# Softcap attention and a maxout MoE on one core: a new order of work, with each attention visit in one piece and all weight subtractions on VectorE

## The chip, the cores and the metric

The kernel runs on one core of one Trainium2 chip. The time is the device time of one execution in microseconds (us); the number before the change is the median of three runs. Engines are named as in the profile: PE is TensorE (PEld its weight loads), DVE is VectorE, ACT is ScalarE, POOL is GpSimd, SP is SyncE.

## What is computed

```python
def _attn_ref(q, k, v, cap):                       # (8, 12, 448, 64) each
    scale = 1.0 / np.sqrt(q.shape[-1])
    scores = scale * np.matmul(q, k.transpose(0, 1, 3, 2))
    scores = cap * np.tanh(scores / cap)           # cap = 30
    scores = scores - np.max(scores, axis=-1, keepdims=True)
    attn = np.exp(scores)
    attn = attn / (np.sum(attn, axis=-1, keepdims=True) + 1e-09)
    return np.matmul(attn, v).astype(np.float32)

def _moe_ref(x, w1, w2, w_out):                    # x: (3584, 768), w1, w2: (768, 1024)
    h1 = x @ w1
    h2 = x @ w2
    g = np.maximum(h1, h2)
    return (g @ w_out).astype(np.float32)          # w_out: (1024, 768)
```

The attention's output, heads side by side, is the x of the second part.

## The kernel before, in words

**The algebra.** max(h1, h2) is relu(x (w1 - w2)) + x w2, so the second part is relu(x wd) w_out + x wm with wd = w1 - w2 and wm = w2 w_out. wd is made by six subtractions, one for each chunk of 128 rows (`subtract`, L354; step `sub`). wm is made by transposing w2 on PE (`W`, L368; copied by `WC`, L372) and multiplying it with w_out (`OP`, `P`, L383; copied by `PC`, L389).

**The attention** works on 48 pairs of heads i = 0..47. Two pairs, 2t and 2t + 1, make a visit t = 0..23, four heads. For each pair, three passes of scores (`S i j`, L466) fill one of two score tiles s0 and s1 in PSUM with 128 keys x two heads x 448 queries; ACT reads the tile with a tanh (`T i j`, L471, 128x896) and then takes the exponent in place in pieces of one, two or three passes (`E i j0 j1`, L488). The last 64 keys of all four heads are one pass of the visit (`L`, L480), with a tanh (`TL`, L484) and an exponent (`EL`, L491). The maximum is not subtracted. The values are `VL t` (last keys, L552) and `V t u j0 j1` (L558), where u is the half of the head's 64 columns. They accumulate in a score tile too, so the tile is taken until the result is normalized. The denominators: DVE adds the exponents of the three passes and the rest (`A t ab j`, L500, and `B t half`, L505), PE sums them over the keys (`Y t`, L525; the first three visits sum all exponents on PE, L518 and L522), and DVE turns, inverts and turns back (`Y1`, `Y2`, `Y3`, L530 to L536) and multiplies into xT (`N t 0`, L570, and twice in `N t 1`, L573). `Y` uses one of four `mm` banks of PSUM.

**The second part** runs over 120 groups, 30 for each pair of batches: `stage1` (8 for each batch, six chunks of wd, evicted with a relu by DVE, L622) and `stage2` (14 halves for a pair of batches, 14 chunks each, copied to osb by DVE, L658, or near the end by ACT, L656). A group opens with `O g bank`. `M x y n` does n steps, each one 64-row half of a chunk of group x in the lower half of the rows of PE and one of group y in the upper half, side by side (L597). `M g g n` takes whole chunks (L592). A group has to change from its one half to its other by a hand-over: an empty instruction on SP (`Hs g`) or DVE (`H g`) waits for the first half's last matmul, and the group's next half waits for it. `ev g` evicts a group (`eva g` on ACT), `st b t` stores an output tile from SP.

**Loads.** POOL issues all loads but the first two, in its order of the list: `lk`, `lq`, `lv` (k, q, v), `lw1`, `lw2`, `lwo` (weights; w1 arrives as f32, in the memory of later osb tiles for chunks 0 to 3 and of a later xT tile for 4 and 5). For the first ten pairs PE transposes q and k (`X`, L410, copied by `XC`, L415); afterwards SP does so with a DMA (`cr t`, L427). There are two buffers each of the loaded q and k, of the transposed ones and of v. `D` are matmuls on a tile of zeros that keep PE going until data come (L423).

**The order of the work** is the string ORDER: its steps are executed as they stand, so it is each engine's queue, in order. An engine waits for data and for free buffers by semaphores and never overtakes its own queue. Nothing else in the program sets an order.

Of the kernel before, what the change touches and what calls it, by code (L numbers as in the profile page):

```python
# [9 lines left out]
ld0 k; ld0 q; ms0; dm; cd k; lk 1 0; lq 1 0; lw2 3; lk 2 0; lw2 2; id; lq 3 0; lq 2 0; lw2 0; lw2 1; lk 3 0;  # L10
D 3 16; cd q; D 3 15; Xh 0 0 0; Xh 0 1; D 3 4; XCh 0 0; XCh 0 1; D 3 4; S 0 0; D 3 5; S 0 1; D 3 4; T 0 0; T 0 1;
D 3 4; S 0 2; D 3 12; X 1 1; D 3 16; W 3 2; XC 1; ms; WC 3; L 0; T 0 2; E 0 0 3; TL 0; S 1 2; D 3 8; X 2 2; S 1 0;
D 3 8; W 2 0; D 3 4; T 1 2; T 1 0; S 1 1; E 1 2 3; T 1 1; XC 2; S 2 1; D 3 1; W 1 3; X 3 2; S 2 0; W 0 1; lk 4 0;
lq 4 0; lwo 0 0; lwo 0 1; lv 0 0; lv 0 1; lk 6 0; lwo 1 0; lwo 1 1; lq 5 0; lv 1 1; lk 7 0; lq 6 0; lk 5 0; lw2 5;
lq 7 0; lv 1 0; T 2 1; T 2 0; WC 1; XC 3; WC 2; WC 0; L 1; X 4 2; S 2 2; OP 2 0 0; P 2 0 1; OP 1 0 1; P 1 0 3;
OP 0 0 3; P 0 0 2; P 1 0 1; P 0 0 1; P 2 0 1; P 0 0 1; P 2 0 2; P 1 0 1; P 2 0 3; P 1 0 3; P 2 0 1; TL 1; EL 0;
T 2 2; EL 1; E 1 0 2; XC 4; PC 2 0; PC 1 0; S 3 0; VL 0; V 0 1 0 2; Y 0 0; V 0 0 0 3; V 0 1 2 3; Y1 0; Y2 0; Y3 0;
N 0 1; N 0 0; T 3 0; E 2 0 3; S 3 1; OP 2 1 2; P 2 1 2; OP 1 1 0; P 1 1 1; OP 0 1 1; P 0 1 1; P 0 0 1; P 1 1 2;
P 0 1 3; P 0 0 2; P 2 1 2; P 1 1 1; P 0 0 1; S 3 2; T 3 1; E 3 0 2; T 3 2; S 4 0; P 0 1 2; P 1 1 2; P 0 1 2;
P 2 1 3; P 1 1 1; S 4 1; T 4 0; E 3 2 3; T 4 1; PC 0 1; PC 0 0; S 4 2; X 5 1; OP 3 0 3; P 3 0 2; P 2 1 1; P 1 1 1;  # L20
XC 5; PC 2 1; PC 1 1; L 2; W 5 1; T 4 2; TL 2; VL 1; V 1 0 0 1; Y 1 0; V 1 0 1 3; V 1 1 0 3; S 5 0; Y1 1; Y2 1;
WC 5; Y3 1; lv 2 1; lw2 4; lk 8 0; lq 9 0; lq 8 0; lw1 0; lw1 2; lk 9 0; lv 2 0; E 4 0 3; T 5 0; X 6 0; XC 6;
N 1 0; N 1 1; P 3 0 3; S 5 1; OP 3 1 2; P 3 1 1; W 4 0; P 3 0 3; P 3 1 7; S 5 2; EL 2; T 5 1; E 5 0 2; T 5 2;
WC 4; PC 3 1; PC 3 0; sub 0 0; S 6 0; OP 4 0 0; P 4 0 8; X 7 3; S 6 1; PC 4 0; XC 7; sub 2 0; T 6 0; E 5 2 3;
T 6 1; S 6 2; X 8 2; X 9 0; L 3; T 6 2; TL 3; Y 2 3; VL 2; S 7 0; V 2 1 0 1; EL 3; T 7 0; XC 8; XC 9; Y1 2; lw1 1;
lw1 5; lk 10 1; lw1 3; lw1 4; lk 12 1; lk 10 0; lq 11 0; lv 3 0; sub 5 1; lv 3 1; lk 11 0; lk 11 1; lq 10 0;
V 2 1 1 2; V 2 0 0 3; V 2 1 2 3; OP 5 0 3; P 5 0 1; OP 4 1 0; P 4 1 2; OP 5 1 2; P 5 1 1; S 7 1; P 4 1 2; P 5 1 3;
P 4 1 1; P 5 1 1; P 5 0 4; P 4 1 1; P 5 0 3; P 5 1 3; P 4 1 2; E 6 0 3; T 7 1; Y2 2; Y3 2; sub 1 0; N 2 1; N 2 0;
sub 3 0; PC 5 0; PC 5 1; sub 4 0; S 7 2; S 8 0; E 7 0 2; T 7 2; T 8 0; O 0 1; M 0 -1 1; O 1 3; M 1 -1 2; M 0 -1 3;
S 8 1; M 0 -1 2; M 1 -1 1; S 8 2; Hs 0; cr 5; T 8 1; T 8 2; E 7 2 3; M 1 0 3; O 2 2; M 2 0 3; L 4; VL 3; A 3 1 1;  # L30
A 3 0 1; A 3 0 2; B 3 0; B 3 1; PC 4 1; A 3 1 2; TL 4; V 3 0 0 3; V 3 1 0 3; Y 3 0; S 9 0; M 2 1 3; ev 0; Y1 3;
Hs 2; EL 4; T 9 0; E 8 0 3; O 3 0; M 3 1 3; M 3 2 3; Hs 3; lv 4 1; lv 4 0; lq 12 0; lv 5 0; lk 13 0; lk 13 1;
lk 12 0; lq 13 0; lk 15 0; lv 6 3; lv 5 2; lk 14 1; lk 15 1; lq 14 0; lk 14 0; lv 5 3; lq 15 0; lv 5 1; S 9 1;
O 4 1; M 4 2 3; M 4 3 3; Y2 3; Y3 3; ev 1; N 3 0; ev 2; T 9 1; Hs 4; O 5 3; M 5 3 3; M 5 4 3; O 6 2; M 6 4 3;
ev 3; N 3 1; A 4 0 1; ev 4; Hs 5; M 6 5 3; O 7 0; M 7 5 2; S 10 0; Hs 6; M 7 5 1; M 7 6 1; S 9 2; M 7 6 2; Hs 7;
cr 6; E 9 0 2; T 10 0; T 9 2; E 9 2 3; O 8 1; M 8 6 3; S 10 2; M 8 7 3; S 10 1; A 4 1 1; ev 5; A 4 0 2; H 8;
B 4 1; B 4 0; A 4 1 2; ev 6; T 10 1; T 10 2; O 9 3; M 9 7 3; M 9 8 5; L 5; M 9 8 2; VL 4; V 4 1 0 2; Y 4 2;
V 4 0 0 3; V 4 1 2 3; TL 5; E 10 0 3; ev 7; Y1 4; Y2 4; Y3 4; N 4 1; N 4 0; S 11 0; M 9 8 4; O 10 0; M 10 8 3;
Hs 9; Hs 8 2; T 11 0; EL 5; M 10 9 3; M 8 9 2; S 11 1; M 8 9 4; S 11 2; M 8 9 2; O 11 2; M 11 9 1; T 11 1; T 11 2;
E 11 0 2; M 11 9 2; S 12 0; M 11 10 5; S 12 1; M 11 10 6; T 12 1; T 12 0; E 11 2 3; A 5 0 1; ev 8; O 12 1;  # L40
M 12 10 3; cr 7; Hs 11; H 10 2; A 5 1 1; ev 9; A 5 0 2; B 5 1; B 5 0; M 12 11 3; M 10 11 1; L 6; M 10 11 2;
S 12 2; M 10 11 5; ev 10; A 5 1 2; TL 6; T 12 2; O 13 3; M 13 11 3; S 13 0; M 13 12 4; VL 5; Y 5 0; V 5 1 0 3;
V 5 0 0 3; T 13 0; E 12 0 3; M 13 12 4; S 13 1; M 13 12 3; lv 6 0; lk 17 0; lv 6 1; lk 16 0; lk 17 1; lv 7 0;
lv 7 3; lq 16 0; lq 17 0; lk 16 1; lk 19 1; lv 6 2; Y1 5; Y2 5; Y3 5; N 5 0; N 5 1; ev 11; T 13 1; EL 6; E 13 0 2;
Hs 13; O 14 0; M 14 12 3; M 14 13 1; S 14 0; M 14 13 2; Hs 12 2; Hs 14; S 13 2; M 12 13 8; O 15 2; M 15 13 3;
M 15 14 3; T 13 2; T 14 0; E 13 2 3; A 6 0 1; A 6 0 2; ev 12; A 6 1 1; ev 13; Hs 15; st 0 1; cr 8; O 16 1;
M 16 14 1; S 14 1; M 16 14 2; M 16 15 3; O 17 3; M 17 15 3; S 14 2; T 14 1; T 14 2; B 6 1; H 16; ev 14; B 6 0;
A 6 1 2; ev 15; M 17 16 3; O 18 0; M 18 16 3; L 7; VL 6; V 6 1 0 3; Y 6 2; V 6 0 0 3; TL 7; S 15 0; M 18 17 3;
lv 8 2; lk 19 0; lq 19 0; lv 7 1; lk 18 1; lq 18 0; lk 18 0; lv 8 1; lk 21 0; lk 20 1; lk 20 0; lv 7 2; lv 8 3;
lk 21 1; ev 16; Y1 6; Y2 6; Y3 6; N 6 0; Hs 18; O 19 2; M 19 17 3; M 19 18 3; ev 17; N 6 1; EL 7; T 15 0;  # L50
E 14 0 3; Hs 19; S 15 1; O 20 1; M 20 18 3; M 20 19 3; O 21 3; M 21 19 3; S 15 2; ev 18; A 7 0 1; A 7 0 2; ev 19;
T 15 1; E 15 0 2; T 15 2; Hs 20; st 0 0; M 21 20 3; Hs 21; S 16 0; O 22 0; M 22 20 3; M 22 21 3; O 23 2;
M 23 21 3; Hs 22; cr 9; ev 20; A 7 1 1; ev 21; M 23 22 6; S 16 1; M 23 22 5; O 24 1; M 24 22 3; T 16 0; E 15 2 3;
T 16 1; B 7 0; H 23; H 22 2; B 7 1; A 7 1 2; S 16 2; M 24 23 3; M 22 23 1; L 8; T 16 2; TL 8; M 22 23 7; S 17 0;
VL 7; Y 7 3; V 7 1 0 2; V 7 0 0 3; V 7 1 2 3; lv 9 2; lq 21 0; lq 20 0; lv 9 0; lv 8 0; ev 22; Y1 7; Y2 7; EL 8;
T 17 0; E 16 0 3; O 25 3; M 25 23 2; S 17 1; M 25 23 1; M 25 24 4; Y3 7; N 7 1; ev 23; N 7 0; M 25 24 7; O 26 0;
M 26 24 2; st 0 2; Hs 25; M 26 24 1; M 26 25 3; S 17 2; T 17 1; E 17 0 2; T 17 2; Hs 24 2; Hs 26; M 24 25 4;
S 18 0; M 24 25 4; O 27 2; M 27 25 3; M 27 26 5; S 18 1; T 18 0; E 17 2 3; T 18 1; M 27 26 1; S 18 2; M 27 26 5;
L 9; A 8 0 1; A 8 0 2; ev 24; A 8 1 1; B 8 1; B 8 0; A 8 1 2; ev 25; T 18 2; TL 9; O 28 1; M 28 26 3; VL 8;
V 8 0 0 1; Y 8 3; V 8 1 0 3; V 8 0 1 3; S 19 0; M 28 27 3; E 18 0 3; T 19 0; Y1 8; cr 10; st 1 3; Hs 26 2; Hs 28;  # L60
M 26 27 8; O 29 3; M 29 27 3; S 19 1; EL 9; T 19 1; Y2 8; Y3 8; N 8 0; N 8 1; A 9 0 1; ev 26; A 9 0 2; ev 27;
S 19 2; M 29 28 8; S 20 0; M 29 28 3; O 30 0; M 30 28 3; Hs 29; Hs 28 2; lk 23 0; lk 22 0; lq 23 0; lk 23 1;
lk 22 1; lq 22 0; lv 9 3; lv 9 1; M 30 29 3; T 19 2; E 19 0 2; T 20 0; E 19 2 3; Hs 30; cr 11; M 28 29 8; S 20 1;
O 31 2; M 31 29 3; S 20 2; M 31 30 3; A 9 1 1; B 9 1; ev 28; ev 29; B 9 0; H 31; A 9 1 2; T 20 1; T 20 2; O 32 1;
M 32 30 3; M 32 31 3; Y 9 3; L 10; VL 9; V 9 1 0 2; V 9 0 0 3; V 9 1 2 3; E 20 0 3; TL 10; ev 30; Y1 9; Y2 9;
Y3 9; st 1 6; Hs 32; O 33 0; M 33 31 3; M 33 32 2; S 21 0; M 33 32 1; O 34 3; M 34 32 3; EL 10; T 21 0; N 9 0;
N 9 1; ev 31; ev 32; Hs 33; lk 25 0; lq 25 0; lv 10 0; lv 10 1; lk 25 1; lk 24 1; lv 11 0; lk 24 0; lq 24 0;
lv 10 2; lv 10 3; lk 26 1; lv 11 3; S 21 2; M 34 33 3; S 21 1; O 35 2; M 35 33 3; Hs 34; st 1 5; T 21 2; T 21 1;
E 21 0 2; M 35 34 3; Hs 35; O 36 1; M 36 34 3; M 36 35 3; S 22 1; S 22 0; ev 33; ev 34; A 10 0 1; A 10 0 2; Hs 36;
# [665 lines left out]
```

## Time and profile before

| | |
|---|---|
| median of 3 runs | 332.95 us (332.04 to 333.63) |
| profiled execution: its time | 335.05 us |
| profiled execution: span of its instructions | 333.3 us |
| granted TensorE clock, mean | 0.992 |
| busy: PE, DVE, ACT, POOL | 325.7, 240.1, 284.4, 164.8 us |
| first tanh starts | 7.14 us |
| VL of visits 3, 4, 22, 23 start | 58.1, 70.9, 284.8, 293.7 us |

Stretches and lines are read from the profiled execution, in us from its first instruction. A busy time is a union of instructions on one engine. Matmuls are pipelined and the ends that the profile gives them are modelled, so PE's busy time is no measure of how well it is used; starts of matmuls are. In the form 64*128 64x384, the first pair is the rows and columns of the array that the matmul takes, the second its moving operand. Line numbers are those of the kernel before.

### The profile page before, as it was taken

Reading aid. Unit: us, or ns where it says so; the run is one execution under the profiler, and the core shown is the slowest. Engines: PE = TensorE matmul, PEld = TensorE weight load, DVE = VectorE, ACT = ScalarE, POOL = GpSimd, SP = SyncE. Lnnn points to the kernel's source line nnn. Section 1 sums busy time; section 2 is a strip of 40 time slices with the busy share of each in tenths; the row PEclk is TensorE's granted clock in tenths of the full one; section 3 lists DMA queues with packets and bytes.
Section 4 is the critical chain, followed back from the end, with each engine's and each line's share of the span. In section 5 each row is a group of like instructions: output and inputs, shape, how many; then the busy total and the mean of one; then the engine's idle time right before and its main releaser. Section 6 shows DMA issues by size and latency. Waiting matters only on the chain.

```text
span 333.3 us, 9760 instructions
## 1 busy us (share of the span) xinstructions
PE 325.7 (98%) x4137; PEld 189.2 (57%) x4139; DVE 240.1 (72%) x421; ACT 284.4 (85%) x276; POOL 164.8 (49%) x240
## 2 busy tenths in 40 slices
PE   8999998999999999999999999999999999999995
PEld 3555552555656555555655565555465555557872
DVE  1346899796886887877897769968897878973201
ACT  3999996999999999999999999999999999941120
POOL 7655583762665960685595566393717532000000
PEclk9999997999999999999999999999999999999998
DMA  8999999899799999999999989699989999100136
GB/s 134 203 201 190 221 265 144 65 132 115 61 151 181 141 182 156 148 133 149 155 132 166 138 140 163 155 136 138 182 115 96 143 137 185 38 2 2 47 96 190
DMA packets 134507, 46.05 MB, mean 138 GB/s; under 512 B 112320, under 2 KB 129472, under 8 KB 134464
## 3 DMA queue, kind: packets, MB, share of 16 engines
q0 software_dynamic: 94880, 25.25, 75.6%
q1 hardware_dynamic: 39280, 19.77, 26.9%
q8 instruction: 32, 0.52, 0.6%
q10 hardware_dynamic: 304, 0.43, 0.4%
q14 instruction: 11, 0.09, 0.1%
HBM read 47.78 MB, written 11.01 MB: 176 GB/s over the span
## 4 chain that ended last, share of the span: by engine, by line
PE 84%; DVE 8%; DMA 3%; ACT 2%; issue 1%; POOL 0%; DVEq 0%
PE mm L597 56%; PE s L558 8%; PE s L466 7%; DMA osb<-in_moe_w_dram 3%; PE mm L383 3%; PE s L480 2%; DVE gT L622 2%; PE s L552 2%; PE mm L525 2%; DVE xT L573 1%; PE mm L592 1%; PE mm L423 1%; ACT e L471 1%; PE mm L410 1%; DVE esum L500 1%
## 5 line engine op out<-in xcount | busy, mean ns | idle before, releaser
L471 ACT ACTIVATE e<-s 128x896 bf16<-128x896 f32 x144 | 127.1, 916 | 8.7 <-PE s L466 6.8
L488 ACT ACTIVATE e<-e 128x1792 bf16<-128x1792 bf16 (+2 forms) x72 | 122.2, 1698 | 0.7
L597 PE MATMUL mm<-wo_sb,gT 64*128 64x384 bf16 x864 | 115.6, 323 | 0.0
L597 PE MATMUL mm<-wm_sb,xT 64*128 64x384 bf16 x648 | 103.6, 323 | 0.2
L597 PE MATMUL mm<-xT,wd_sb 64*128 64x448 bf16 x768 | 100.9, 353 | 1.3 <-DVE wm_sb L389 0.9
L597 PEld LDWEIGHTS <-gT 64*128 64x128 bf16 x864 | 59.1, 94 | 25.7 <-issue 2.3
L597 PEld LDWEIGHTS <-wd_sb 64*128 64x128 bf16 x768 | 50.1, 95 | 29.4 <-issue 5.2
L292 POOL DMA_DIRECT2D kqs<-in_k_dram x76 | 54.7, 723 | 13.2 <-DMA qkT<-kqs 10.2
L597 PEld LDWEIGHTS <-xT 64*128 64x128 bf16 x648 | 49.9, 94 | 19.8 <-issue 3.1
L466 PE MATMUL s<-qkT 64*128 64x448 bf16 x288 | 53.4, 353 | 0.5 <-DVE xT L570 0.4
L316 POOL DMA_DIRECT2D vp<-in_v_dram x48 | 30.7, 642 | 44.8 <-PE s L558 20.8
L622 DVE TENSOR_SCALAR gT<-mm 128x448 bf16<-128x448 f32 x64 | 38.7, 618 | 12.1 <-PE mm L597 11.7
L316 POOL DMA_DIRECT2D vl<-in_v_dram x38 | 23.6, 623 | 34.7 <-PE s L552 29.7
L292 POOL DMA_DIRECT2D kqs<-in_q_dram x38 | 35.3, 929 | 6.4 <-issue 6.4
L558 PE MATMUL s<-e,vp 128*32 128x448 bf16 x576 | 35.4, 354 | 0.0
L658 DVE COPY osb<-mm 128x384 f32<-128x384 f32 x44 | 23.9, 555 | 14.5 <-PE mm L597 13.7
L573 DVE TENSOR_TENSOR xT<-s,inv 64x448 bf16<-64x448 f32 x48 | 29.9, 622 | 1.4
L500 DVE TENSOR_TENSOR esum<-e 128x896 bf16<-128x896 bf16 x42 | 25.6, 616 | 6.6 <-PE mm L597 4.0
L500 DVE TENSOR_TENSOR esum<-esum,e 128x896 bf16<-128x896 bf16 x42 | 26.1, 623 | 3.0 <-PE s L466 0.6
L505 DVE TENSOR_TENSOR esum<-esum,el 64x896 bf16<-64x896 bf16 x42 | 26.0, 619 | 2.4 <-PE mm L597 1.3
L656 ACT COPY osb<-mm 128x384 f32<-128x384 f32 x10 | 4.8, 479 | 26.0 <-PE mm L597 25.7
L466 PEld LDWEIGHTS <-qkT 64*128 64x128 bf16 x288 | 17.0, 94 | 17.1 <-issue 6.8
(57 smaller groups left out, 268.6 us busy)
## 6 DMA issues: line engine op xcount, KB each, us to landing
out_dram<-osb SPq DMA_DIRECT2D x54, 192.0 KB, 3.4
vp<-in_v_dram POOLq DMA_DIRECT2D x38, 160.0 KB, 4.1
kqs<-in_q_dram POOLq DMA_DIRECT2D x47, 112.0 KB, 4.4
kqs<-in_k_dram POOLq DMA_DIRECT2D x76, 56.0 KB, 3.9
osb<-in_moe_w_dram POOLq DMA_DIRECT2D x4, 512.0 KB, 9.4
gT<-in_moe_w_dram POOLq DMA_DIRECT2D x6, 256.0 KB, 6.7
wo_sb<-in_moe_w_out_dram POOLq DMA_DIRECT2D x4, 384.0 KB, 8.4
vp<-in_v_dram POOLq DMA_DIRECT2D x10, 128.0 KB, 5.6
```

The source lines that it names most:

```text
L292: nc.gpsimd.dma_start(out=to, in_=x)
L316: nc.gpsimd.dma_start(out=to, in_=x)
L466: scored[i, j] = nc.tensor.matmul(s[:, h, :S], k_of(t, o, h, j), q_of(t, o, h)).ins
L471: nc.scalar.activation(expo[i][:, 2 * j : 2 * j + 2, :], slots[i, j][:, :, :S], AF.Tanh, scale=scale / cap)
L488: nc.scalar.activation(e, e, AF.Exp, scale=float(cap))
L500: nc.vector.tensor_add(d, e[:, 0:2, :] if j == 1 else d, e[:, 2 * j : 2 * j + 2, :])
L505: nc.vector.tensor_add(d, d, left_e[t][r, :, :])
L558: nc.tensor.matmul(vals[t][place(m, u), u, :S], w[:, m, :], expo[2 * t + o][:, 2 * j + h, :], start=False, stop=(j == NJ - 1))
L573: nc.vector.tensor_mul(x[64 - r : 128 - r], vals[t][r : r + 64, u, :S], sums[t, 3][64 - r : 128 - r])
L597: ins = nc.tensor.matmul(self.ps, w[r], x[r], start=first, stop=self.at == [self.n, self.n]).ins
L622: nc.vector.tensor_relu(gT[b // 2][:, f, cs], ps)
L658: nc.vector.tensor_copy(o[:, hs], ps)
```

## The change

Only ORDER changes. Both lists have the same steps, with the same n in sum for `M`, `P` and `D` and the same tanh and exp pieces, except that

- `sub 5 1` (the subtraction of chunk 5 on POOL) becomes `sub 5 0` (on DVE),
- the hand-over `H 47` is gone,
- the `V` passes are cut in other places (`V t u 0 2` and `V t u 2 3` in place of mixed pieces).

What moves: in the first part (to visit 5) the order of the loads, of the warm matmuls, of the premultiplication and of the six subtractions is new, and the constants of ones are filled first (`ms` ahead of `dm`). From visit 5 to 22, `L t+1`, `VL t`, `V t 0 0 2`, `V t 1 0 2`, `Y t`, `V t 0 2 3`, `V t 1 2 3` follow each other on PE (in some visits with one MoE step ahead of `Y`), the scores come after them, and the MoE steps come in ones and twos between all other steps; each load of the middle stands by itself between them instead of in a burst. The tail has the same steps with some evictions and stores at other places.

The first part, its beginning and the steps about the subtractions:

```diff
-ld0 k; ld0 q; ms0; dm; cd k; lk 1 0; lq 1 0; lw2 3; lk 2 0; lw2 2; id; lq 3 0; lq 2 0; lw2 0; lw2 1; lk 3 0;
-D 3 16; cd q; D 3 15; Xh 0 0 0; Xh 0 1; D 3 4; XCh 0 0; XCh 0 1; D 3 4; S 0 0; D 3 5; S 0 1; D 3 4; T 0 0; T 0 1;
...
-WC 5; Y3 1; lv 2 1; lw2 4; lk 8 0; lq 9 0; lq 8 0; lw1 0; lw1 2; lk 9 0; lv 2 0; E 4 0 3; T 5 0; X 6 0; XC 6;
...
-lw1 5; lk 10 1; lw1 3; lw1 4; lk 12 1; lk 10 0; lq 11 0; lv 3 0; sub 5 1; lv 3 1; lk 11 0; lk 11 1; lq 10 0;
...
-P 4 1 1; P 5 1 1; P 5 0 4; P 4 1 1; P 5 0 3; P 5 1 3; P 4 1 2; E 6 0 3; T 7 1; Y2 2; Y3 2; sub 1 0; N 2 1; N 2 0;
-sub 3 0; PC 5 0; PC 5 1; sub 4 0; S 7 2; S 8 0; E 7 0 2; T 7 2; T 8 0; O 0 1; M 0 -1 1; O 1 3; M 1 -1 2; M 0 -1 3;
...
+ld0 k; ld0 q; ms0; ms; dm; cd k; D 3 16; lq 1 0; lk 2 0; lq 2 0; lk 1 0; lw2 3; id; lw2 2; lw2 1; lq 3 0; lw2 0;
+lk 3 0; lwo 0 0; lwo 0 1; cd q; D 3 16; Xh 0 0 0; Xh 0 1; XCh 0 0; XCh 0 1; D 3 8; S 0 0; T 0 0; S 0 1; D 3 16;
...
+Y1 1; lk 8 0; lk 6 0; lq 8 0; lv 1 0; lq 7 0; lq 6 0; lw2 4; lw1 4; lv 5 2; lw1 0; lk 9 0; lw1 2; lv 2 1; lv 5 3;
+lq 9 0; lv 2 0; L 2; P 2 1 1; W 5 1; VL 1; V 1 1 0 1; V 1 0 0 3; V 1 1 1 3; TL 2; E 4 0 3; S 5 0; X 6 0; P 2 1 2;
...
+X 7 3; OP 4 0 0; P 4 0 5; P 3 1 1; lk 11 1; lw1 5; lw1 1; lw1 3; lv 3 1; lk 10 0; lv 3 0; lq 10 0; lk 10 1;
+lk 11 0; lq 11 0; XC 7; sub 0 0; PC 3 1; P 4 0 1; Y 2 3; L 3; P 4 0 2; S 6 2; TL 3; T 6 2; Y1 2; Y2 2; Y3 2;
+PC 4 0; sub 2 0; OP 5 0 3; P 5 0 3; S 7 0; X 8 2; X 9 0; VL 2; V 2 1 0 3; V 2 0 0 3; T 7 0; E 6 0 3; XC 9; XC 8;
+N 2 1; N 2 0; sub 5 0; S 7 1; P 5 0 2; OP 5 1 2; P 5 1 2; OP 4 1 0; P 4 1 1; P 5 0 3; P 4 1 2; P 5 1 2; O 0 1;
+M 0 -1 1; S 7 2; T 7 1; E 7 0 2; T 7 2; PC 5 0; sub 1 0; sub 3 0; S 8 0; P 5 1 4; P 4 1 4; S 8 1; O 1 3; M 1 -1 1;
+T 8 0; T 8 1; M 1 -1 2; S 8 2; M 0 -1 5; L 4; Hs 0; cr 5; T 8 2; EL 3; TL 4; E 7 2 3; M 1 0 3; P 4 1 1; PC 5 1;
```

A visit of the middle (13):

```diff
-T 28 1; E 27 2 3; M 53 52 5; L 14; M 53 52 1; S 28 2; M 53 52 5; H 53; A 13 1 2; TL 14; T 28 2; S 29 0; O 54 3;
-M 54 52 3; M 54 53 3; VL 13; V 13 1 0 2; V 13 0 0 1; Y 13 2; V 13 0 1 3; V 13 1 2 3; T 29 0; E 28 0 3; lk 32 1;
-lk 32 0; lq 32 0; lk 33 1; lv 15 2; lv 14 3; lv 14 0; lv 15 1; lk 33 0; lq 33 0; lk 35 0; lq 34 0; lv 15 3;
-lk 35 1; lq 35 0; lk 34 0; lk 34 1; H 52 2; Y1 13; Y2 13; M 52 53 1; S 29 1; M 52 53 7; O 55 2; M 55 53 3;
-M 55 54 1; Y3 13; N 13 0; N 13 1; ev 52; ev 53; M 55 54 8; S 29 2; M 55 54 2; O 56 0; M 56 54 3; T 29 1; EL 14;
...
+M 53 52 2; A 13 1 1; M 53 52 2; cr 15; M 53 52 1; T 28 1; M 53 52 1; B 13 0; S 28 2; M 53 52 2; B 13 1; O 54 3;
+M 54 52 1; T 28 2; M 54 52 2; H 53; M 54 53 1; H 52 2; E 27 2 3; M 54 53 2; M 52 53 1; L 14; VL 13; A 13 1 2;
+TL 14; V 13 0 0 2; V 13 1 0 2; Y 13 2; E 28 0 3; V 13 0 2 3; lk 34 0; V 13 1 2 3; Y1 13; S 29 0; M 52 53 1;
+lv 15 0; M 52 53 1; Y2 13; M 52 53 2; Y3 13; M 52 53 1; lv 15 1; M 52 53 2; O 55 2; M 55 53 1; N 13 0; M 55 53 1;
+lv 15 2; M 55 53 1; T 29 0; M 55 54 1; N 13 1; M 55 54 2; lv 15 3; M 55 54 2; EL 14; M 55 54 1; S 29 1; lk 34 1;
+M 55 54 2; ev 52; M 55 54 1; T 29 1; S 29 2; lq 34 0; M 55 54 1; ev 53; M 55 54 1; O 56 0; M 56 54 1; T 29 2;
```

## The prediction

> **What bounds the kernel now.** I read the page first, then the busy times by stretch, then the timeline of PE, the chain of waits and the groups by shape.
>
> ```profile
> PE 325.7 (98%) x4137; PEld 189.2 (57%) x4139; DVE 240.1 (72%) x421; ACT 284.4 (85%) x276; POOL 164.8 (49%) x240
> PEclk9999997999999999999999999999999999999998
> ```
>
> PE looks full, but its ends are modelled, so I count columns instead. The stretches (my cuts: the left pass VL of visit 4 starts at 70.9 us, that of visit 22 at 284.8):
>
> ```profile
> core 0: us, PE busy (x) PEld busy (x) DVE busy (x) ACT busy (x) POOL busy (x), PEclk, DMA share, GB/s
> 0.00:70.90 70.90, 67.69 (x862) 34.52 (x864) 48.17 (x84) 62.52 (x61) 45.09 (x73) 0.98 1.12 174
> 70.90:284.80 213.90, 213.62 (x2769) 123.80 (x2768) 173.07 (x306) 207.70 (x198) 119.72 (x168) 1.00 1.20 144
> 284.80:333.30 48.50, 44.37 (x523) 30.92 (x507) 18.81 (x33) 14.18 (x19) 0.00 (x0) 0.98 0.21 58
> ```
>
> The middle is 18 visits of 11.88 us. The timeline of PE in it shows the pace:
>
> ```profile
> 187.59 0.32 PE L597 MATMUL mm<-wm_sb,xT 64*128 64x384 bf16 x1
> 187.75 0.32 PE L597 MATMUL mm<-wo_sb,gT 64*128 64x384 bf16 x1
> 188.82 0.39 PE L480 MATMUL s<-qkT 64*32 64x448 bf16 x8
> 189.02 0.38 PE L552 MATMUL s<-el,vl 64*32 64x448 bf16 x8
> 189.32 0.37 PE L558 MATMUL s<-e,vp 128*32 128x448 bf16 x4
> 189.53 0.72 PE L525 MATMUL mm<-esum,ones 128*32 128x448 bf16 x4
> ```
>
> A pair of halves starts every 0.16 us (384 columns), so 448 columns take 0.187. The middle holds 1178 halves of 384 (589 pairs, 94.2 us), 576 of 448 (288 pairs, 53.9), 216 halves of scores (108, 20.2), 432 value matmuls, four side by side (108, 20.2), and 18 each of Y, L and VL at 0.187 (10.1): 198.6 us of columns in 213.9. So 15.3 us, 0.85 a visit, are lost. Part of it is changes of shape: L to VL (both 64*32) follow 0.20 us apart, 0.01 over their columns, but VL to V (64*32 to 128*32) 0.30, 0.11 over. From V to Y (both 128*32) there is 0.02. I take 0.12 for a change; the list of before has 71 in the middle, 8.5 us. The other 6.8 us (0.38 a visit) are waits and uneven pairs.
>
> ACT is close behind. In runs without a wait (two tanh in 1.73 us, one 0.92) a tanh of 896 follows the last by 0.81, and by the starts an exp of 896 takes 0.84, of 1792 1.59 and of 2688 2.33, so a visit costs 7 x 0.81 + 2.33 + 0.84 + 1.59 + 0.84 = 11.3 us, 203 for 18. The middle is bound by PE, with ACT 5% under it. After visit 23's VL (293.7 us) come 39.6 us, nearly all MoE matmuls that nothing can shorten.
>
> **The first stretch** has one hole:
>
> ```profile
> 45.99 2.14 POOL L354 TENSOR_TENSOR wd_sb<-xT,gT 128x1024 bf16<-128x1024 f32 x1
> 46.05 3.17 DVE L354 TENSOR_TENSOR wd_sb<-osb,gT 128x1024 bf16<-128x1024 f32 x1
> 51.06 1.22 DVE L354 TENSOR_TENSOR wd_sb<-osb,gT 128x1024 bf16<-128x1024 f32 x1
> 53.12 1.22 DVE L354 TENSOR_TENSOR wd_sb<-xT,gT 128x1024 bf16<-128x1024 f32 x1
> ```
>
> The subtractions feed the first MoE matmuls. One stood 3.17 us instead of 1.22 beside POOL's, the last ended at 54.3. Meanwhile ACT idled 0.23 + 0.80 + 0.59 + 1.02 = 2.6 us (its row's gaps at 51 to 58). The granted clock was 0.73 in 54:56 and 0.50 in 56:58.
>
> **The change, part by part.** Both lists hold the same instructions except one: the subtraction of chunk 5 (POOL 2.14) becomes DVE (1.22), and one empty hand-over on DVE (H 47) goes. So busy sums stay; only order moves.
>
> *Subtractions.* DVE gains 1.22 us and loses the 1.95 us of standing: -0.7 us on its chain 46 to 54.
>
> *First part.* (a) The four memsets of ones move ahead of the warm tile: 0.11 + 0.11 + 0.28 = 0.5 us on DVE, so the 32 warm blocks (8 x 0.43 us, against 31 before) start about 0.5 later and the first tanh at 7.6 rather than 7.14: +0.4. What hid them was DVE's idle time at 10.5. (b) w1 chunk 4 and its w2 chunk move to the front of the w1 loads, and chunks 4, 0, 2 are subtracted early. Loads land in the order of POOL's list, one after another (w1 chunk 3 issued at 37.0 lands at 47.3, chunk 4 issued at 40.0 at 48.5), so the order sets when the last one lands. After has the same loads ahead of its last w1 (chunk 3) and two small ones of v more, 0.6 us each by the spacing of such landings: 48.5 + 1.2 = 49.7, less what POOL's standing at 28.7 to 31.5 for a transpose gives back. One subtraction follows it: the end at 51 instead of 54.3. (c) By the list VL of visit 3 stands behind 46.9 us of ACT work (cut at its own exp): 7.6 + 46.9 + about 1 of small waits = 55.5, against 58.1. So the first stretch gains 2.6; bounds: -4 (hole and half clock all gone) to +2 (the +0.4, plus a scores pass late behind a w2 transpose or warm block, 0.5 to 1.5).
>
> On the half clock: at 56:58 the row says 0.50. The Trainium skill, "TensorE: Matmul & The Clock Gate", "The HAM clock gate", says that a window of about 3.4 us without enough activity halves the clock, binary; the trace agrees (0.50). By that rule the hole costs another 1.7 us, which comes back only if no idle of such a length is left; it is inside the bound of -4.
>
> *Middle.* Now L, VL, V, Y and V follow each other, and M steps come in ones and twos. By the lists there are 60 changes of shape instead of 71: 11 x 0.12 = 1.3 us. The Trainium skill, "TensorEngine Tiling (Array Packing)", "Key Properties", says that a change of tiling mode, not of tile, drains TensorE; by its wording V to Y costs nothing, as here (0.02), and the gain would be the same 11 drains.
>
> The other 0.38 us a visit decide. I walk visit 13, from the scores pass S 28 2 on PE at 0. Its tanh starts at 0.40 (a scores pass's second half to its tanh, shortest) or, if the tanh before still runs, up to 0.80; the exp of 896 starts 0.80 later and takes 0.95; the add A 13 1 2 needs 0.03 + 0.62: ready at 2.8 to 3.2. PE reaches Y after 0.19 + 9 steps (1.44) + L, VL (0.37) + 2 changes (0.24) + 16 V matmuls (0.75) = 3.0. It fits, or PE stands 0.2. From the last Y matmul to the last N are 4.0 us (the usual value in before: 0.40 to the first transpose, then 3.6 of DVE); PE has V, a change, S 29 0, 16 steps, S 29 1 and 3 steps before S 29 2, which needs the N: 3.9 to 4.1. It fits to 0.1. H 53 stands on DVE behind B 13 1, and PE's next half of group 53 waits for it. From Y1 at 3.45 DVE has 1.6 + 1.9 (N) + 6 evictions and 5 adds at 0.57 = 9.8 us, ends at 13.2, less a period of 11.5: 1.7; PE comes at 1.2. That is up to 0.5 of standing, in visits whose H lies there.
>
> So the plan is tight at three points and its floor is (198.6 + 60 x 0.12) / 18 = 11.43 us, over ACT's 11.3. Bounds for the middle: all waits gone, -1.3 - 6.8 = -8.1; waits doubled, +5.5. Between them I take waits cut by a fifth (0.38 to 0.31): -1.3 - 1.2 = -2.5, near the row of before since DVE and ACT are as full as they were.
>
> *Loads and SP.* The loads of the middle go one by one instead of in bursts. POOL idles 30 us for value matmuls there and 10 for transposes, so it is early; 10 issues of 0.6 to 0.9 us a visit leave 4 us. Zero; if that cover fails, a late load costs its 4 us landing once a visit. Stores and crossings share SP with the hand-overs; the number is the same. Zero.
>
> *End.* After VL 23 the same steps follow; the last two groups run one after the other instead of interleaved, the last copy still follows the last matmul. Zero.
>
> **Sum**, against the profiled execution (span 333.3, time 335.05, so 1.75 around): 335.05 - 2.6 - 2.5 = 329.95. The median of the runs is 2.1 below that execution, so 327.9 for the median: 328.0.
>
> **Rivals.** A, *the middle reaches its floor*: 332.95 - 2.6 - 8 = 322. For it: every wait in the walk fits to 0.2 us. Against: nothing in before reaches it. Chance 0.2. Forecast (324 to 331.3): 0.42. B, *no difference*: pieces save the 1.3 us of shape changes, and the hole merely moves (the loads bound it): 331.3 to 334.6, say 332. Seven of 18 L and VL already stood together, so little is changed. Chance 0.16. C, *slower*: the piece makes PE stand for VectorE. Y right behind its own add, and H behind B, leave no other matmul to run. Price: 18 visits x wait; it decides when the wait grows from 0.38 to more than 0.38 + (1.3 + 2.6)/18 = 0.60 us a visit; with 0.9 (0.5 at H on top): 332.95 - 3.9 + 9.4 = 338. For it: DVE's 9.8 us chain; against: not every visit has its H there. Chance 0.22.
>
> Half a per cent (1.7 us) is about what a measurement of this kernel can tell from no change. Faster 0.62, within 0.16, slower 0.22. The range 320 to 337 leaves out the far ends of A and C.
>
> **What would show it.** First tanh at 7.6; the last subtraction's end near 51, no subtraction on POOL, granted clock 1.00 in the fifties; VL 3 near 55.5. VL 4 to VL 22 near 211.4, with L to VL 0.20 apart everywhere. Wrong, if the group Y or the halves of L597 show idle time released by DVE, if the tanh row waits longer for scores than its 3.4 us in the middle, or if VL 3 comes later than 58.

## The result

The kernel after takes 330.02 us (median of 5 runs, 329.21 to 330.89), the kernel before 333.63 (5 runs, 332.04 to 334.19): ratio 0.988, 95% interval 0.984 to 0.992. The forecast was 328.0, in a range of 320 to 337, with faster at 0.62. The direction held and the time lies 2.0 us above the forecast: 4.95 us off 332.95 were forecast, and 3.6 us off 333.63 were measured.

The profiled execution of after took 330.89 us, with a span of 329.1, where that of before had 335.05 and 333.3. The page's busy times and granted clock, and the stretches, cut at VL of visits 4 and 22 as for before:

```profile
PE 321.2 (98%) x4136; PEld 184.3 (56%) x4138; DVE 240.5 (73%) x422; ACT 280.6 (85%) x276; POOL 161.6 (49%) x239
PEclk9999999999999999999999999999999999999998
```

```profile
core 0: us, PE busy (x) PEld busy (x) DVE busy (x) ACT busy (x) POOL busy (x), PEclk, DMA share, GB/s
0.00:68.90 68.90, 65.01 (x859) 32.93 (x861) 46.92 (x83) 61.57 (x60) 41.25 (x69) 1.00 1.18 178
68.90:280.00 211.10, 211.10 (x2774) 123.67 (x2771) 174.95 (x308) 205.18 (x198) 120.37 (x170) 1.00 1.29 147
280.00:329.20 49.20, 45.04 (x529) 27.68 (x513) 18.66 (x32) 13.80 (x19) 0.00 (x0) 0.98 0.22 57
```

Against before the first stretch is 2.0 us shorter (70.9 to 68.9), the middle 2.8 (213.9 to 211.1), and the end 0.7 longer (48.5 to 49.2; from VL of visit 23 on, 39.6 to 39.9). But these cuts don't part the same work. By the two lists, after has ten MoE halves of 384 columns fewer ahead of VL 4, four more between VL 4 and VL 22 and six more behind it, four of them behind VL 23. At the 0.16 us that a pair takes that is 0.8, 0.3 and 0.5 us, so for the same work the first stretch is 1.2 shorter, the middle 3.1, and the end 0.2 longer. DVE's busy time stayed (240.1 and 240.5) and ACT's is 3.8 us less for the same 276 instructions; the lists hold the same work, so what was gained is order, as the text on record had it.

VectorE's queue of after about the subtractions (L390 here; the lines of after are 36 further down than those of before):

```profile
46.00 1.20 DVE L390 TENSOR_TENSOR wd_sb<-osb,gT 128x1024 bf16<-128x1024 f32 x1
...
48.51 1.26 DVE L609 TENSOR_TENSOR xT<-s,inv 64x448 bf16<-64x448 f32 x2 [0.25 <-PE s L594]
49.78 0.62 DVE L606 TENSOR_TENSOR xT<-s,inv 128x448 bf16<-128x448 f32 x1
50.32 1.22 DVE L390 TENSOR_TENSOR wd_sb<-xT,gT 128x1024 bf16<-128x1024 f32 x1
51.45 0.55 DVE L425 CAST wm_sb<-mm 128x384 bf16<-128x384 f32 x1
51.92 2.35 DVE L390 TENSOR_TENSOR wd_sb<-osb,gT 128x1024 bf16<-128x1024 f32 x2
```

No subtraction takes longer than 1.22 now, and still the last one (the second of the 2.35) ends at 54.27, where before's ended at 54.34. It isn't waiting for data: w1's last chunk landed at 49.2. Ahead of the first product VectorE waits 0.25 us for TensorE's value matmuls; from there on each row starts where the one before ends, so it is VectorE's own queue that is late. The hole on TensorE is gone none the less, because the new list keeps premultiplication matmuls back for it (eight of them start between 51.4 and 52.9 in the timeline). Busy times of 52 to 54 and of 56 to 58 in after, columns as in the stretches:

```profile
52.00:54.00 2.00, 2.00 (x15) 0.80 (x13) 2.00 (x3) 2.00 (x3) 0.27 (x1) 1.00 2.34 145
56.00:58.00 2.00, 2.00 (x31) 0.84 (x33) 1.85 (x4) 1.90 (x3) 0.00 (x0) 1.00 0.78 178
```

TensorE is busy 2.00 of 2.00 in both, and the clock is 1.00.

The middle, in the timeline of PE of after, one visit's left pass to its next scores:

```profile
174.20 0.38 PE L516 MATMUL s<-qkT 64*32 64x448 bf16 x8
174.40 0.37 PE L588 MATMUL s<-el,vl 64*32 64x448 bf16 x8
174.70 0.94 PE L594 MATMUL s<-e,vp 128*32 128x448 bf16 x16
175.47 0.36 PE L561 MATMUL mm<-esum,ones 128*32 128x448 bf16 x4
175.66 0.55 PE L594 MATMUL s<-e,vp 128*32 128x448 bf16 x8
176.14 0.36 PE L502 MATMUL s<-qkT 64*128 64x448 bf16 x2
176.34 0.32 PE L633 MATMUL mm<-wo_sb,gT 64*128 64x384 bf16 x1
```

The starts are what to read. L to VL are 0.20 apart (columns 0.187: nothing lost), VL to V 0.30 (0.11 lost), V to Y to V nothing (16 value matmuls, four side by side, are 0.75; Y starts 0.77 behind them), V to scores 0.48 for 0.375 of columns (0.11 lost), scores to MoE nothing. So a visit now pays for three changes of shape, the third being the one from MoE to L.

### The profile page after: what moved, and what is told of

Read it like the earlier page. It is cut to its first block, busy times and chain, and to the rows that moved or that the text cites. A ratio compares the mean times of both kernels' runs of the same rounds, so it can differ in the third digit from the quotient of the medians.

```text
span 329.1 us, 9769 instructions
## 1 busy us (share of the span) xinstructions
PE 321.2 (98%) x4136; PEld 184.3 (56%) x4138; DVE 240.5 (73%) x422; ACT 280.6 (85%) x276; POOL 161.6 (49%) x239
## 2 busy tenths in 40 slices
DMA packets 134507, 46.05 MB, mean 140 GB/s; under 512 B 112320, under 2 KB 129472, under 8 KB 134464
## 4 chain that ended last, share of the span: by engine, by line
PE 90%; DMA 4%; DVE 3%; POOL 2%; issue 0%; POOLq 0%; DVEq 0%
PE mm L633 60%; PE s L502 9%; PE s L594 9%; PE mm L419 4%; DMA wo_sb<-in_moe_w_out_dram 4%; PE s L516 2%; PE mm L561 2%; PE s L588 1%; PE mm L628 1%; DVE wd_sb L390 1%; POOL kqs L321 1%; PE mm L446 1%; DVE esum L536 1%; POOL gT L370 1%; PE mm L554 1%; DVE wm_sb L425 0%
## 5 line engine op out<-in xcount | busy, mean ns | idle before, releaser
L507 ACT ACTIVATE e<-s 128x896 bf16<-128x896 f32 x144 | 125.2, 924 | 7.5 <-PE s L502 7.3
L633 PE MATMUL mm<-wm_sb,xT 64*128 64x384 bf16 x648 | 102.3, 323 | 0.0
L633 PE MATMUL mm<-xT,wd_sb 64*128 64x448 bf16 x768 | 97.1, 349 | 0.0
L633 PEld LDWEIGHTS <-wd_sb 64*128 64x128 bf16 x768 | 48.9, 94 | 26.6 <-issue 2.0
L502 PE MATMUL s<-qkT 64*128 64x448 bf16 x288 | 51.9, 352 | 0.6 <-ACT e L507 0.4
L609 DVE TENSOR_TENSOR xT<-s,inv 64x448 bf16<-64x448 f32 x48 | 29.9, 622 | 1.1 <-PE s L594 0.2
L502 PEld LDWEIGHTS <-qkT 64*128 64x128 bf16 x288 | 18.4, 94 | 20.8 <-issue 12.5
L566 DVE STREAM_TRANSPOSE st<-mm 128x448 f32<-128x448 f32 x24 | 15.6, 649 | 13.3 <-PE mm L561 11.4
```

The lines of the kernel that those rows point to most:

```text
L502: scored[i, j] = nc.tensor.matmul(s[:, h, :S], k_of(t, o, h, j), q_of(t, o, h)).ins
L507: nc.scalar.activation(expo[i][:, 2 * j : 2 * j + 2, :], slots[i, j][:, :, :S], AF.Tanh, scale=scale / cap)
L609: nc.vector.tensor_mul(x[64 - r : 128 - r], vals[t][r : r + 64, u, :S], sums[t, 3][64 - r : 128 - r])
L633: ins = nc.tensor.matmul(self.ps, w[r], x[r], start=first, stop=self.at == [self.n, self.n]).ins
```

## The experiments

Ratios are against runs of the kernel before on the same chip, with the 95% interval; "VL 3" is the start of VL of visit 3. Where a list is joined or cut, the rest is word for word the list named.

**The subtraction alone, in the old order.** Kernel before, with

```diff
-sub 5 1;
...
-N 2 0; sub 3 0;
+N 2 0; sub 5 0; sub 3 0;
```

> The kernel before, with the subtraction of chunk 5 on DVE (between N 2 0 and sub 3 0) instead of POOL; nothing else. Theory (DVE's queue of subtractions and normalizations sets the end of the hole at 54): chunk 1 takes 1.2 us instead of 3.2, chunk 5 adds 1.2, so the last subtraction ends 0.7 earlier, near 53.6, VL 4 starts 0.7 earlier, and the time falls by about 0.7 us (0.2%). Rival 1 (the landing of w1 sets the hole): no change. Rival 2 (the hole is what lowers the granted clock, and a slightly shorter one does not): granted clock 1.00 in the fifties and 2 to 2.5 us less.

333.44 us, ratio 0.9997 (0.9974 to 1.002): no difference that can be measured. VectorE from the first subtraction's start to the last one's end, in before and in this kernel:

```profile
40.21:54.34 14.13, 12.55 (x190) 6.32 (x188) 14.02 (x19) 13.03 (x14) 10.51 (x13) 1.00 1.34 230
```

```profile
40.09:53.36 13.27, 12.46 (x190) 6.29 (x188) 13.16 (x20) 12.88 (x14) 8.39 (x12) 1.00 1.23 226
```

In both, VectorE is busy all but 0.1 us, so its queue sets the end of the subtractions here too. It is 0.86 us shorter (14.13 to 13.27): the text on record had 0.7. The last subtraction ends at 53.36 (53.6 was expected) and VL 4 starts at 68.9. Worth 0.3% at most, it is less than the runs can show.

**The subtraction back on GpSimd, in the new order.** Kernel after, with

```diff
-N 2 1; N 2 0; sub 5 0;
+N 2 1; N 2 0; sub 5 1;
```

> The changed kernel, with the subtraction of chunk 5 back on POOL, where DVE's stood in the list; nothing else. Theory (the matmuls of the premultiplication that the new list keeps back cover the wait for the subtractions): within 0.5 us of the changed kernel, 329.5 to 330.5, granted clock still 1.00. Rival (the move to DVE is what closed the hole): 0.7 to 2.5 us more than the changed kernel and a granted clock under 1.00 in the fifties.

329.37 us, ratio 0.9877 (0.9848 to 0.9906), that of after. The two subtractions that meet, in its timeline:

```profile
48.91 2.14 POOL L396 TENSOR_TENSOR wd_sb<-xT,gT 128x1024 bf16<-128x1024 f32 x1
49.82 3.46 DVE L396 TENSOR_TENSOR wd_sb<-osb,gT 128x1024 bf16<-128x1024 f32 x2
```

GpSimd's ends at 51.05. VectorE's (the first of the two in its row), issued at 49.82, ends 1.09 us behind that, 2.32 instead of 1.22 after its start. What GpSimd takes off VectorE's queue, VectorE loses again by standing: from the first subtraction's start to the last one's are 12.40 us here and 12.42 in after. "All subtractions on VectorE" is worth nothing that these runs can tell in this order.

**The two halves of the list.** One kernel with after's list up to `L 5` (not with it) and what is left of before's list behind it, and one the other way round.

```diff
 (after's list up to) L 5;
-(after's rest)
+(before's list, without the steps already done)
```

> The new list up to L 5, then the old list without what is done already: the first part alone. Theory (first part and middle each bring their own share): VL 4 at 69 as in the changed kernel, then 214 us to VL 22 as in before, time 2.0 us under before (ratio 0.994). Rival (the middle of before cannot use the earlier start, or only the middle brings the gain): VL 22 at 284.8 as in before, ratio 1.00.

333.62 us, ratio 1.0005 (0.9972 to 1.0037). The expectation failed: the new first part in front of the old middle brings nothing that can be measured. In the profile VL 3 and VL 4 are early, at 54.8 and 68.5, but visit 4, the first behind the seam, then takes 13.0 us instead of 12.3, and VL 4 to VL 22 214.8 instead of 213.9. So 0.9 us is given back, most of it where old and new order meet. And the lead of 2.4 us at VL 4 is one over before's profiled execution, with its half clock; the next kernel shows what that is worth.

> The old list up to L 5, then the new list without what is done already: the middle (and the end) alone. Theory: VL 4 at 70.9 as in before, then 211.1 us to VL 22 as in the changed kernel, time 2.5 us under before (ratio 0.992), the two parts adding up to the whole change. Rival (the pieces only work from the changed kernel's start): 214 us between VL 4 and VL 22, ratio 1.00.

331.55 us, ratio 0.9933 (0.9908 to 0.9959), as expected: the new middle by itself is worth 2.2 us, with 211.0 from VL 4 to VL 22. What the new first part adds to it is the step from 0.9933 to 0.9878, some 1.8 us by these two ratios, whose intervals overlap. This kernel has before's first part, hole and all. The rows of 52 to 54 and 56 to 58, of before and then of this kernel:

```profile
52.00:54.00 2.00, 1.21 (x7) 0.47 (x6) 2.00 (x4) 1.33 (x2) 1.25 (x2) 1.00 1.56 140
56.00:58.00 2.00, 2.00 (x17) 0.61 (x21) 1.89 (x5) 1.39 (x2) 0.00 (x0) 0.50 0.87 198
```

```profile
52.00:54.00 2.00, 1.29 (x7) 0.47 (x6) 2.00 (x4) 1.24 (x2) 1.17 (x2) 1.00 1.62 144
56.00:58.00 2.00, 2.00 (x46) 0.95 (x43) 1.91 (x4) 1.97 (x4) 0.00 (x0) 1.00 0.92 209
```

TensorE is busy 1.29 of 2 us, much as in before's hole, and the granted clock stays at 1.00, where before's profile has 0.50. So the hole doesn't halve the clock in every execution. Each run lists its mean clock: of the 59 executions of the kernel before that were run beside the experiments, 16 had 0.995 or less (median 335.2 us, without two above 338) and 43 more than that (median 333.7). This kernel had it in 2 of 12, the first experiment in none of 12, and kernels with the new first part in none of 57. The profiled execution of before (335.05 us, 0.992) was one of that first kind; a half clock of the 3.4 us that its trace shows (54.9 to 58.3) is 0.005 of the mean. That the other executions had their drop at the same place isn't shown, they have no trace; but only kernels with the old first part had it, and it costs about 1.4 us in about a quarter of before's executions.

It also explains the kernel ahead of this one. VL 4 stands at 69.6 here, with two MoE steps fewer ahead of it than in before; with them it would be 69.9, by 0.16 each. Of the 2.4 us that the new first part was early at VL 4 in front of the old middle, 1.0 was thus the half clock of before's profiled execution, by one profile each, and 0.9 is given back. The 0.5 us that are left are less than those runs can tell.

**Two changes of shape more in each visit.** Kernel after, with `L 5` to `L 22` each moved ahead of the MoE step before it, so that the step stands between L and VL, for example

```diff
-M 13 11 1; ev 10; L 6; VL 5;
+L 6; M 13 11 1; ev 10; VL 5;
```

> The changed kernel, with L of each of the visits 5 to 22 moved one MoE step ahead, so that a step stands between L and VL. Theory (the middle is full of PE work, and each change of shape costs 0.12 us): two changes more a visit, less the 0.01 between L and VL, 18 x 0.24 = 4.3 us: 215.4 us from VL 4 to VL 22, time 4.3 over the changed kernel (ratio to before 1.000). Rival (ACT sets the pace and PE has 0.2 us a visit to spare): within 1 us of the changed kernel (ratio 0.988 to 0.991).

333.27 us, ratio 0.9967 (0.9944 to 0.9989). The middle:

```profile
67.80:282.10 214.30, 214.30 (x2774) 125.04 (x2772) 175.06 (x308) 206.42 (x198) 120.39 (x170) 1.00 1.21 144
```

214.3 where after has 211.1: +3.2 us. 17 of the 18 moved steps lie between these two starts, so that is 34 changes of shape more, 0.09 us each where 0.12 was expected. Most of what is added on TensorE's row comes through to the time, against the rival, so TensorE sets the middle.

**Constants late.** Kernel after, with `ms` (the ones) moved from ahead of the warm tile to behind `XC 1`, where before has it.

```diff
-ms0; ms; dm;
+ms0; dm;
...
-XC 1; WC 3;
+XC 1; ms; WC 3;
```

> The changed kernel, with the constants of ones filled where before fills them (behind XC 1) instead of ahead of the warm tile. Theory: the first tanh starts 0.4 to 0.8 us earlier, and since ACT's work is what the first part waits for, the whole kernel ends as much earlier: 329.4 or a little under (ratio to before 0.987). Rival (the loads and subtractions set the first part): VL 4 and the time unchanged.

329.55 us, ratio 0.9857 (0.9825 to 0.9889): near the theory's 329.4, but after's 330.02 lies inside the interval too, so the time doesn't decide. The first tanh starts at 6.59 instead of 7.53. VL 3 at 55.4 is 0.9 earlier in this one profile, but it is 37.3 us behind the first premultiplication matmul (L419 of after) in both. The start itself differs from execution to execution: the first tanh of the kernels with after's order of the start stood between 6.96 and 7.82. Six of them have VL 3 at 54.7 to 55.3, ahead of this kernel's 55.4, with a later tanh. So the traces speak against an effect of the first tanh on what follows.

**ScalarE relieved, VectorE relieved.** Kernel after, one with the exponentials of the passes over half of the queries, one with two adds over half.

```diff
+        e = e[:, :, : S // 2]
         nc.scalar.activation(e, e, AF.Exp, scale=float(cap))
```

> The changed kernel with the exponents of the three passes on half of the queries only (the other half keeps its tanh): ACT's work in a visit falls by about 2.4 us to 8.9. Theory (the middle is at PE's own floor): 210 to 211 us from VL 4 to VL 22, the first part shorter. Rival (ACT sets the pace of the middle, PE waits for it 0.2 to 0.3 us a visit): 205 to 208 us.

```diff
+        if j == 2:
+            d, e = d[:, :, : S // 2], e[:, :, : S // 2]
         nc.vector.tensor_add(d, e[:, 0:2, :] if j == 1 else d, e[:, 2 * j : 2 * j + 2, :])
...
-        nc.vector.tensor_add(d, d, left_e[t][r, :, :])
+        d = d[:, :, : S // 2]
+        nc.vector.tensor_add(d, d, left_e[t][r, :, : S // 2])
```

> The changed kernel with the third add and the add of the last keys of each pair on half of the queries only (the denominators lack the rest): DVE's work in a visit falls by about 1.2 us. Theory (no wait for DVE is left on PE's path in the middle): 210 to 211 us from VL 4 to VL 22. Rival (Y behind its add and the hand-over behind the adds make PE stand 0.3 us a visit): 205 to 207 us.

The middles of the two:

```profile
67.30:278.10 210.80, 210.80 (x2772) 126.36 (x2771) 175.51 (x309) 169.35 (x198) 120.36 (x170) 1.00 1.25 147
```

```profile
67.50:278.10 210.60, 210.60 (x2772) 123.95 (x2771) 158.67 (x308) 204.95 (x198) 120.29 (x170) 1.00 1.23 147
```

The kernels took 329.01 and 328.91 us, in one run each. ScalarE's busy time falls from 205.2 to 169.4 and the middle by 0.3 us; VectorE's falls from 175.0 to 158.7 and the middle by 0.5 (seven kernels with this middle as it stands have 211.0 to 211.1). So relief of either alone is worth 0.5 us at most; both together weren't tried. And VL 3 stands 37.1 us behind the first premultiplication matmul with 6 us less of ScalarE's work between 19 and 55, where kernels with all their work and the same loads have 36.9 to 37.3: ScalarE doesn't set the first part either, against what the prediction built on.

**What sets the first part: w_out's landing?** After's chain of waits begins with the load of w_out's first half (7.13 to 18.94), so I moved one w2 chunk of 256 KB ahead of it, and in another kernel one behind it.

```diff
-lk 3 0; lwo 0 0; lwo 0 1;
+lk 3 0; lw2 5; lwo 0 0; lwo 0 1;
...
-lv 1 1; lw2 5; lq 5 0;
+lv 1 1; lq 5 0;
```

> The kernel after, with one more load (the sixth block of w2, 256 KB) put into GpSimd's queue ahead of w_out's first half, and nothing else changed. Theory (the first part is set by the landing of w_out's first half, and by TensorE's and VectorE's unbroken work from there): in the first 55 us of the kernel after the transfers moved 195 GB/s, so 256 KB more ahead is 1.3 us. The first matmul of L419 goes from 19.0 to 20.3, the first VL of visit 3 and all after it 1.3 us later, ratio to the kernel before 0.992 where the kernel after has 0.988. Rival (another chain, of ACT's or VectorE's work, sets the first part, and the landing has slack): the premultiplication begins later, but VL of visit 3 stands within 0.4 us of where it was against the first tanh, ratio 0.988.

```diff
-lw2 3; id;
+id;
...
-lwo 0 0; lwo 0 1; cd q;
+lwo 0 0; lwo 0 1; lw2 3; cd q;
...
-D 3 23; W 3 2; T 0 1; T 0 2; XC 1; WC 3;
+D 3 23; T 0 1; T 0 2; XC 1;
...
-Y 0 0;
+W 3 2; WC 3; Y 0 0;
```

> The kernel after, with one load (the fourth block of w2, 256 KB) moved from ahead of w_out's first half to behind it, and the turning of that block on TensorE moved to where a bank is free after the first fifteen microseconds of premultiplication. Theory (the landing of w_out's first half sets the first part): the first matmul of L419 goes from 19.0 to 17.7, VL of visit 3 from 56.3 to 55.0, the time from 330.0 to 328.7, ratio 0.984. Rival (what stands next to it is late: keys, queries, the other blocks of w2 and the exponentials, or the turned block now takes TensorE 0.8 us in the part that is without gaps): VL of visit 3 gains less than 0.4 us, ratio 0.987 to 0.989.

330.45 us, ratio 0.9901 (0.987 to 0.9933), and 330.14, ratio 0.9889 (0.9857 to 0.9922): neither differs from after. The load of w_out in the chains of waits of after and of the kernel with 256 KB more ahead of it (start, us, what):

```profile
7.13 11.81 DMA wo_sb<-in_moe_w_out_dram
```

```profile
7.90 10.07 DMA wo_sb<-in_moe_w_out_dram
```

It is issued 0.8 later and lands 1.0 earlier, but that shows nothing: in the nine kernels that have after's loads ahead of it, one profile each, this load lands anywhere between 16.8 and 18.9. Its landing scatters by more than the 1.3 us that was to be added, so this kernel doesn't decide. In the kernel that moves it forward the first matmul stands at 17.4, and VL 3 38.4 us behind it where the others with all their work have 36.9 to 37.3: the turning of the w2 chunk (0.6 to 0.8 us on TensorE by such groups in after) now lies where TensorE is full. That an earlier start was eaten by this work, as the rival had it, fits; one profile is no proof.

**TensorE relieved, then TensorE and ScalarE.** From 19 to 55 us after has TensorE busy for 35.96 of 36, ScalarE for 35.64. Kernel after with seven of eight premultiplication matmuls over half of the columns, then with the halved exponentials as well.

```diff
-                ps, w2T[c][:, f * P : (f + 1) * P], wo_sb[:, f, hs], start=(f == 0), stop=(f == FC - 1)
+                ps[:, : DM // 4] if f else ps, w2T[c][:, f * P : (f + 1) * P],
+                wo_sb[:, f, hs.start : hs.start + DM // 4] if f else wo_sb[:, f, hs], start=(f == 0), stop=(f == FC - 1)
```

> The kernel after, in which seven of the eight matmuls of each premultiplication (L419) go over half of w_out's columns; every instruction, load and wait stays. It leaves out part of the product of w2 and w_out. Theory (from the landing of w_out's first half on, TensorE's unbroken work sets the first part): 84 matmuls lose 192 of 384 columns, 0.08 us each by the 0.16 us that 384 take, 6.7 us in all, nearly all of it ahead of VL of visit 3, which stood 37.3 us behind the first matmul of L419. It comes earlier until the next thing sets it: the last chunk of w1 landed at 49.2, its subtraction takes 1.2 and the last keep of the product and VL 3.2 more, near 53.6; so VL of visit 3 between 49.6 and 53.6, 34.5 us or less behind the first matmul of L419. Rival (w1's loads and VectorE's queue set it already): VL of visit 3 stays within 0.6 us of 37.3 behind that matmul, and TensorE's busy time in 35 to 55 falls from 20.0 of 20 by what is taken off.

> The kernel after, with seven of eight premultiplication matmuls over half of the columns and with the exponentials of the passes over half of the queries; every instruction, load and wait stays. It leaves out part of the product of w2 and w_out and half of the probabilities. Theory (TensorE and ScalarE are both full from 19 to 55, 35.96 and 35.64 us of 36, so that relief of one alone leaves the other): VL of visit 3, which stood 37.3 us behind the first matmul of L419 in the kernel after, 37.1 with the exponentials halved and 36.6 with the matmuls halved, now comes 35.0 or less behind it; of the 5 us that TensorE and the 6 us that ScalarE lose at least 2 come through, until the last chunk of w1 or VectorE's queue is next. Rival (VectorE's queue and w1's loads set it in all of these kernels): it stays at 36.0 to 37.3.

The first took 329.46 us and the second 328.88, in one run each. VL 3 stands 36.6 us behind the first premultiplication matmul with TensorE relieved (its busy time in 19 to 55 fell by 4.9 us), 36.5 with both, so the relief is worth 0.3 to 0.7 us. The theory that two full engines hold each other fell; the rival held, if with a little more than its 0.6 us in the first kernel. From the first subtraction's start to the last one's end, in after and in the kernel with both relieved:

```profile
40.63:54.27 13.64, 13.64 (x198) 6.43 (x196) 13.25 (x20) 13.61 (x14) 8.89 (x13) 1.00 1.54 213
```

```profile
39.17:52.54 13.37, 11.74 (x196) 6.39 (x192) 13.17 (x20) 11.15 (x14) 9.06 (x13) 1.00 1.45 217
```

TensorE goes from 13.64 to 11.74 of busy time, ScalarE from 13.61 to 11.15, VectorE keeps its 13.2, and that stretch is 13.64 and 13.37 us long. VectorE's queue has one gap of note there, the 0.25 us ahead of the first product in after (0.11 with both relieved); all others are 0.05 or less. In after and in nine other kernels with the new first part, the halved exponentials and the halved matmuls among them, VL 3 stands 15.6 to 15.7 us behind the first subtraction, and 15.3 with both halved. So from 39 us on it is the queue of VectorE, full even where TensorE and ScalarE have gaps, that is left to set the first part (the halved adds left it as it was: none of them lies in there). Ahead of that the first subtraction stands 21.6 us behind the first premultiplication matmul in after, 21.3 to 21.6 in seven other kernels that do all that work there or lack only ScalarE's, and 21.0 and 21.3 in the two kernels here. In that piece TensorE waits for ScalarE if it alone is relieved (2.4 us of 3.2). What it waits for with both relieved, its timeline says in brackets (idle time, and what ended it; three of the seven waits):

```profile
23.39 0.39 PE L590 MATMUL s<-el,vp 64*32 64x448 bf16 x8 [0.19 <-DMA vp<-in_v_dram]
26.26 1.40 PE L419 MATMUL mm<-wo_sb,w2T 128*128 128x384 bf16 x12 [1.04 <-DMA wo_sb<-in_moe_w_out_dram]
30.76 0.41 PE L447 MATMUL mm<-ident,kqs 64*64 64x64 bf16 x14 [0.28 <-DMA kqs<-in_q_dram]
```

Loads: v, the second half of w_out, q; they are 1.9 of the 2.5 us. So from the first premultiplication to 39 us the loads are just behind the engines, and from there on VectorE. No kernel here relieves either of these two, so that they set the first part is argued from the timelines, and how much they hold back isn't measured.

## Why the prediction was right in direction and 2.0 us too low

- **What bounds the middle.** Right: 11 changes of shape fewer, and a floor set by TensorE with ScalarE just under it. Relief of ScalarE or VectorE alone gives 0.3 and 0.5 us, one broken pair of L and VL a visit costs 3.2.
- **Middle, -2.5.** Measured -2.8 (-2.9 with before's first part), -3.1 for the same work. A change of shape was taken at 0.12; the starts in the timeline say 0.11, the broken pairs 0.09. So 11 changes fewer are 1.0 to 1.2 us of it. The rest, some 2 us of fewer waits and uneven pairs, was taken at 1.2, a fifth of 6.8, and no row gives a fifth: that it came out near is luck in part, and no run isolates it. (Ten of 18 L and VL stood together in before's list, not seven.) The walk of a visit said "fits, or to 0.1 to 0.2"; some 12 us of the 211.1 are above the columns, near 7 of them changes of shape (60 x 0.11), and up to 0.5 us came from relief of one other engine; the rest has no cause shown. Rival C's standing for VectorE did not come. ScalarE did wait longer for scores than before (3.8 against 3.4), which the text took as a sign against the forecast; the middle gained all the same, since ScalarE doesn't set it.
- **Subtractions, -0.7.** Right as a size in the old order (0.86), worth nothing measurable in the new one.
- **First tanh at 7.6.** It stood at 7.53, but the traces show no path from the +0.4 to the end: with the first tanh at 6.59, VL 3 is where it is in other kernels. The time alone can't tell 0.4 us.
- **Last w1 at 49.7, last subtraction's end at 51.** The landing was right (49.2). The end was the failed step: 54.27. "One subtraction follows it" left out what else is in VectorE's queue between 48.5, where the value matmuls of visit 2 end, and that subtraction: three products with the inverse sums (L609, L606), two more subtractions and a copy, 4.5 us. The rows above show them end to end.
- **VL 3 at 55.5 behind 46.9 us of ScalarE's work.** It stood at 56.3 here and at 54.4 to 55.8 in other kernels with this first part, so the number was near by luck, and the reason wrong: ScalarE's work can shrink by 6 us with no more than 0.2 us gained. After also has six MoE halves fewer ahead of VL 3 than before, which the comparison with 58.1 left out. Summing the work of an engine that looks full gives a bound, and here TensorE was as full.
- **The hole and the half clock.** The hole did go, and the clock was 1.00. The size was about right: 1.7 us by the rule, about 1.4 by the medians. But that was a drop of the clock that before's profiled execution had and three of four executions don't have. The Trainium skill, "TensorE: Matmul & The Clock Gate", "The HAM clock gate", says that the window of activity runs freely and doesn't start with the kernel; that agrees with a hole beside which the mean clock fell in 16 of 59 executions and not in the rest.
- **End, zero.** From VL 23 on it is 0.3 us longer in every kernel with the new remainder (39.9 against 39.6), but two MoE steps more (four halves, 0.3 us) stand behind VL 23 in the new list. For the same work zero was right.
- **The sum.** The span of the profiled executions fell by 4.2 where 5.1 was forecast: first stretch -2.0 for -2.6, middle -2.8 for -2.5, end +0.7 for 0, rounded (-1.2, -3.1 and +0.2 for the same work, and some 1.0 of the -1.2 is the clock). The other 1.2 us is the step to the median: I took 2.1 off the profiled execution, most of which was the dropped clock, and then counted the hole's gain in full against the median as well. After's profiled execution lies 0.9 above its median.

## What to carry to other kernels

Before you price a stall from one profile, look whether the other executions have it: the mean granted clock of each run tells that, and a gain that only the profiled execution could give must not be taken off the median too. When a late step is moved earlier, walk the queue of the engine that issues it, not only the arrival of its data. Two or three engines that are all full make the sum of one a bound, not a forecast: halve the work of one and measure before calling it the limit. And when two orders of work are compared by stretches, count what each list has ahead of the cut: here 0.8 of a gain of 2.0 us and 0.5 of a loss of 0.7 were steps that stand on another side of it.

## What was not expected of the hardware

A subtraction on VectorE with two operands, issued while GpSimd's runs, seems to do its work only when that one ends: it is issued at 46.05 against an end at 48.13 in before, 46.10 against 48.07 with after's rest, 49.82 against 51.05 with GpSimd's put back, and each time the VectorE instruction ends 1.08 to 1.09 us after GpSimd's, for a duration of 3.17, 3.04 and 2.32 instead of 1.22. The Trainium skill, "SBUF — State Buffer", "SBUF: two separate sides", calls it an exclusive lock that the first takes for the whole instruction; these three rows agree.

The same load behind the same loads, the first half of w_out, landed between 16.8 and 18.9 us in the profiled executions of nine kernels. A landing time of one execution is no base for a difference of 1 us. Why it scatters isn't shown.
